# A memory-value chain moved ahead of value loads, weights taken one pair earlier, a comparison moved to GpSimd

## The chip, the cores and the metric

The kernel runs on one core of a Trainium2 chip. Its metric is the device time of one execution, in microseconds (us). Three runs of the kernel before took 1214.63, 1216.63 and 1217.8 us; the median is 1216.63. The profile is of one execution of its own.

## The reference

Two independent layers share the input length of 2048 positions; their outputs are put side by side.

Layer A is a state-space scan: `h = Lam_bar * h + x @ B_bar` over the positions, and `y = 2 * Re(h @ C) + x * D`.

Layer B is attention in 64 segments of 32 positions, with 32 heads of 128 elements and 8 memory rows:

```python
for s in range(n_seg):
    h = concatenate([mem, xs], axis=1)            # 8 memory rows, 32 positions
    q, k, v = h @ Wq, h @ Wk, h @ Wv
    p = softmax(where(mask, q @ k.T * scale, -1e9))
    o = (p @ v) @ Wo
    mem = o[:, :M]                                # the next segment's memory
    outs.append(o[:, M:])
```

The memory rows of a segment come from the segment before. The kernel does not run the segments one after another. It first makes a guess of every segment's memory (`guess`, kept as columns of `b_xe` behind the inputs, called memT), computes all segments with it, and in the end holds statistics gathered on the way (`b_cert`, `b_nrm`, `b_accE`, `b_rall`) against limits; if they do not hold, a general loop is run instead. "Guess comparison" means the part of these statistics that each block of heads adds.

## The kernel before

The work runs in this order; the times are those of the profile.

- To 346 us: values `v = x @ Wv` of all blocks of four heads (hb 0 to 7), interleaved with stage 1 of layer A. Values go to DRAM as `b_vx`.
- 346 to 464 us: stage 2 of layer A, and the guess.
- 464 to about 985 us, the stage of the change: `proj` makes queries and keys for 16 pairs of heads (hp), and `attention` works on one pair while `proj` makes the next. Each pair of heads has 18 projection steps, of eight or 32 matmuls (L578 and L589), and nine attention units, u = 0 to 8. Two projection steps go between two units, and ten go ahead of the first unit. `v_mem(hb)` computes the values of the memory rows once for each block of four heads.
- From 985 us: the output projection with Wo, which runs to the end.

`v_mem` is a generator of three pieces. The first loads the block's weights (wv), multiplies them with memT (32 matmuls, L488), copies the result to `b_vmst` on ScalarE (ACT, L492 by the helper's line 74, and L493), and stores it to DRAM as `b_vm` (L494). The second loads it back transposed as `b_vmr` (L497), squares two things on ACT into `b_wide` (L500, L501), and subtracts them into `b_ct` on VectorE (DVE, L503): this is the guess comparison. The third stores `b_vt` to DRAM (L505) and sums `b_ct` over the partitions on TensorE (`sums`: L515, read out by L516). Block 0 is taken between the first ten projection steps, after those numbered 2, 5 and 8; block hp + 1 is taken during head pair hp, at units 3, 5 and 7.

`load_v(i)` loads, for half i of the units, the values `b_v` (one transfer of 512 KB, L602) and the memory values `b_u` (four of 128 KB, L607, which read `b_vt`). An attention unit scores (L626), takes exponentials on ACT (L628), masks on GpSimd (POOL, L635), multiplies with `b_v` (L666), adds `b_u` on DVE (L668), takes reciprocals (L670), and scales on POOL (L674).

All these transfers are issued on one queue, that of SyncE (SP). Weights of every kind come into one pool of six buffers of 1 MB (`w8`): wqk of a pair (two transfers, L554), wv of a block (L383), and in the stages before those of C and Wo. All projection steps, `v_mem` and `sums` share two PSUM buffers, psP. Copies of queries and keys out of psP are done by DVE and ACT through one helper (lines 74 and 76). At the end of a pair two short steps (L589) are copied by four DVE casts (L592, L593, again line 76).

The order of the instructions on each engine is set when the program is built. A scheduler goes through the traced program and gives each engine its next instruction: the first in program order among those whose inputs and buffer are there. So a load can be issued long before its place in the text. `keep_in_program_order` (`pin` in the code) ties an instruction behind the one that was traced before it on its engine; it is only an order, not a wait.

The loop that drives the stage is this:

```python
pr, at = b.proj(), b.attention()
vm = b.v_mem(0)
for i in range(done):
    next(pr)
    if i in (2, 5, 8):
        next(vm)
```

Of the kernel before, what the change touches and what calls it, by code (L numbers as in the profile page):

```python
# [12 lines left out]
ALU = mybir.AluOpType  # L13
# [13 lines left out]
HB = 8; HP = 16  # L27
# [265 lines left out]
class PartB:  # L293
# [186 lines left out]
    def v_mem(self, hb):  # L480

        k = self.k
        pin = k.tc.keep_in_program_order
        w = self.load_wv(hb)
        p = k.ps("P")
        for h in range(4):
            for c in range(KC):
                k.PE.matmul(p[:, h * NM:(h + 1) * NM], w[:, c, h * 128:(h + 1) * 128], self.memT[:, c, :],  # L488
                            start=(c == 0), stop=(c == KC - 1))
        st = self.vmst[hb % 2]  # L490
        pv = p[:, 0:4 * NM].rearrange("p (h n) -> p h n", h=4)
        k.copy("s", st[:, :, 0:M], pv[:, :, 0:M])  # L492
        k.S.activation(st[:, :, M:NM], pv[:, :, M:NM], ACT.Copy, scale=float(M))  # L493
        pin(k.SP.dma_start(self.vm[hb].rearrange("(h p) n -> p h n", p=128), st[:]))  # L494
        yield
        vr = self.p3.tile([128, 512], BF16, name="b_vmr", bufs=1)
        pin(k.SP.dma_start(vr[:], self.vm[hb][:, :], transpose=True))  # L497
        n = NSEG - 2
        a, b = (self.wide[:, 4 * n * i:4 * n * i + 4 * n].rearrange("p (h n) -> p h n", h=4) for i in range(2))
        k.S.activation(a, self.ogT[:, hb * 4:(hb + 1) * 4, 1:1 + n], ACT.Square, scale=TOL)  # L500
        k.S.activation(b, st[:, :, M:M + n], ACT.Square, scale=1.0 / L)  # L501
        t = self.ct[:, hb % 2, 0:4 * n]
        k.V.tensor_tensor(t.rearrange("p (h n) -> p h n", h=4), a, b, ALU.subtract)  # L503
        yield
        pin(k.SP.dma_start(self.vt[hb][:], vr[0:NM, :]))  # L505
        self.sums(self.ct[:, hb % 2, :], 2 * hb)
        yield
# [42 lines left out]
    def load_wqk(self, hp):  # L550
        if hp < HP:
            w = self.k.w8((2 * KC, 256), "wqk")
            for i in range(2):
                self.k.SP.dma_start(w[:, i * KC:(i + 1) * KC, :], self.Wf[i][:, :, hp * 256:(hp + 1) * 256])  # L554
            self.wqk[hp] = w

    def norm(self, hp, w, i, hh):
# [7 lines left out]
    def proj(self):  # L565

        k = self.k; PE = k.PE
        NS = T + M - XMAIN
        for hp in range(HP):
            self.load_wqk(hp + 1)  # L570
            w = self.wqk.pop(hp)
            for q in range(4):
                for i in range(2):
                    t = self.qk[hp % 2][i]
                    for hh in range(2):
                        p = k.ps("P")
                        for c in range(KC):
                            PE.matmul(p[:, 0:480], w[:, i * KC + c, hh * 128:(hh + 1) * 128], self.xe[:, c, 480 * q:480 * q + 480],  # L578
                                      start=(c == 0), stop=(c == KC - 1))
                        k.copy("s" if i else "v", t[:, hh, M + 480 * q:M + 480 * q + 480], p[:, 0:480])  # L580
                        if q == 1:
                            self.norm(hp, w, i, hh)
                        yield
            for i in range(2):
                t = self.qk[hp % 2][i]
                p = k.ps("P")
                for hh in range(2):
                    for c in range(KC):
                        PE.matmul(p[:, hh * NS:(hh + 1) * NS], w[:, i * KC + c, hh * 128:(hh + 1) * 128], self.xe[:, c, XMAIN:XMAIN + NS],  # L589
                                  start=(c == 0), stop=(c == KC - 1))  # L590
                pv = p[:, 0:2 * NS].rearrange("p (h n) -> p h n", h=2)
                k.copy("v", t[:, :, M + XMAIN:QW], pv[:, :, 0:128])  # L592
                k.copy("v", t[:, :, 0:M], pv[:, :, 128:NS])  # L593
                yield


    def load_v(self, i):
        if i < 2 * HP:
            k = self.k
            hp, half = divmod(i, 2)  # L600
            hb, cs = hp // 2, slice((hp % 2) * 256, (hp % 2) * 256 + 256)
            k.SP.dma_start(self.vb[i % 3][:, :, 1:257], self.vx[hb][1024 * half:1024 * half + 1024, :].rearrange("(g p) n -> p g n", p=128)[:, :, cs])  # L602
            v = self.vt[hb][:, :]
            for j in range(4):
                r = M - 1 + 32 * half + j
                src = bass.AP(v.tensor, v.offset + r * 512 + (hp % 2) * 256, [[0, 32], [4 * 512, NU], [1, 256]])
                k.SP.dma_start(self.ub[i % 3][32 * j:32 * j + 32, :, 1:257], src)  # L607

    def load_vs(self, hb):
        k = self.k  # L610
# [72 lines left out]

    def attention(self):
        units = [(hp, u) for hp in range(HP) for u in range(UPH)]
        self.load_v(0)
        self.load_v(1)
        pend = []
        for n, (hp, u) in enumerate(units):
            if u == 1:  # L690
                self.load_v(2 * hp + 2)
            if u == 3 and hp % 2 == 0:
                self.load_vs(hp // 2)
            if u == 6:
                self.load_v(2 * hp + 3)
            pend.append((hp, u, self.att_front(hp, u)))
            if len(pend) > 2:
                self.att_back(*pend.pop(0))
            yield hp, u
        for p in pend:  # L700
            self.att_back(*p)
            yield HP, 0
# [202 lines left out]
def kernel_main(tc, A_x, A_Lre, A_Lim, A_Bre, A_Bim, A_Cre, A_Cim, A_logdt, A_Dskip, B_x, B_mem0, B_Wq, B_Wk, B_Wv, B_Wo, out,  # L905
                force=False, dbg=None):
    with ExitStack() as ctx:
        k = K(tc, ctx)
# [3 lines left out]
        a = PartA(k, A_x, A_Lre, A_Lim, A_Bre, A_Bim, A_Cre, A_Cim, A_logdt, A_Dskip, out)  # L912
        b = PartB(k, B_x, B_mem0, B_Wq, B_Wk, B_Wv, B_Wo, out)

        def pool(name, side, bufs=2):
            return tc.tile_pool(name=name, bufs=bufs, side=side, reuse_waits="tile")
# [7 lines left out]
        with pool("p1", "right") as p1:  # L924
# [26 lines left out]
            def values():  # L951
                yield from b.v_first(wvs[0], xr, k.SP)
                for hb, q in [(1, 0), (1, 1)] + [(hb, q) for q in range(2, 8) for hb in range(2)]:
                    yield from b.v_pair(hb, q, wvs[hb], k.SP)
                for hb in range(2, HB):
                    for q in range(8):
                        if q == 1 and hb + 1 < HB and hb + 1 not in wvs:
                            wvs[hb + 1] = b.load_wv(hb + 1)
                        yield from b.v_pair(hb, q, wvs[hb], k.SP)
            v = values()  # L960
# [17 lines left out]
            for n in range(PC * NB):  # L978
# [8 lines left out]
                half = done + 2  # L987
# [32 lines left out]
        with pool("p2", "right") as p2:  # L1020
            g = b.guess()
# [17 lines left out]
        with pool("p3", "right") as p3:  # L1039
            b.p3 = p3  # L1040
            b.qk_init(p3)
            pr, at = b.proj(), b.attention()
            vm = b.v_mem(0)
            done = 10
            for i in range(done):
                next(pr)
                if i in (2, 5, 8):
                    next(vm)
            b.wo0, b.acc = [], {}
            early = b.op_some([(0, 0), (1, 0)], range(3), "P", 2)  # L1050
            for n, (hp, u) in enumerate(at):
                if u == 3 and hp < 7:
                    vm = b.v_mem(hp + 1)
                if u in (3, 5, 7) and hp < 7:
                    next(vm)
                if u == 4 and 8 <= hp < 12:
                    w = k.w8((8, 512), "wo0")
                    k.SP.dma_start(w, b.Wo[:, 8 * (hp - 8):8 * (hp - 7), 0:512])
                    b.wo0.append(w)
                if u == 6 and hp in (4, 8, 12):  # L1060
                    b.load_o(0, hp // 4 - 1)
                want = min(18 * HP, 10 + 2 * (n + 1))
                if done == want:
                    for _ in range(2):
                        next(early, None)
                while done < want:
                    next(pr)
                    done += 1
                    if done == 18 * HP:
                        w1 = xep.tile([128, KC, XP], BF16, name="b_xe")  # L1070
                        b.wo1 = w1[:].rearrange("p c n -> p (c n)")[:, 0:H * 512].rearrange("p (h n) -> p h n", h=H)
                        k.SP.dma_start(b.wo1, b.Wo[:, :, 512:D])
            for _ in early:
                pass
# [101 lines left out]
```

## Time and profile before

| | |
|---|---|
| median of three runs | 1216.63 us (1214.63 to 1217.8) |
| the profiled execution | 1214.49 us |
| its span, first to last instruction | 1212.8 us |
| granted TensorE clock, mean | 0.999 |
| TensorE (PE) busy | 1202.6 us |
| VectorE (DVE) busy | 591.1 us |
| ScalarE (ACT) busy | 392.9 us |
| GpSimd (POOL) busy | 323.0 us |
| share of the 16 DMA engines, 464 to 500 us | 0.85 |

How to read the lines shown from here on: in a timeline, a line has its start and its duration in us, the engine, the line of the kernel, the operation, what it writes and reads with shapes, and how many instructions were merged into it; in square brackets stands how long the engine had been idle before it and what ended that. A line of SPq is a transfer's issue on the SP queue, not the transfer. In the waits, a line has the engine and what waited, for what, the us in total, how many times, and the longest.

### The profile page before, as it was taken

How to read it: one execution, taken by the hardware profiler on the slowest of the kernel's cores; microseconds unless marked ns; L12 is line 12 of the kernel's file. 1: busy time of each engine (PE TensorE's matmuls, PEld its weight loads, DVE VectorE, ACT ScalarE, POOL GpSimd, SP SyncE). 2: the span in 40 equal slices, each digit the busy share in tenths (PEclk: the TensorE clock that was granted, in tenths of full speed). 3: DMA queues.
4: the chain of work that ended last, by engine and by line, in shares of the span. 5: the costliest groups of instructions: out<-in, count | busy, mean ns of one | idle time of the engine just before them, and what ended most of it. 6: DMA issues, size and time to landing. Idle time of an engine off the chain costs nothing.

```text
span 1212.8 us, 18965 instructions
## 1 busy us (share of the span) xinstructions
PE 1202.6 (99%) x7592; PEld 621.5 (51%) x7592; DVE 591.1 (49%) x1012; ACT 392.9 (32%) x841; POOL 323.0 (27%) x345
## 2 busy tenths in 40 slices
PE   9999999999999999999999999999999999999998
PEld 4444444444445544555555555555555554444444
DVE  5889999999973333343444344444444440100000
ACT  3444344443320003444444444444444420000000
POOL 1000000000023232455555555555555560000000
PEclk9999999999999999999999999999999999999999
DMA  9932232432666646987678775755575559507000
GB/s 233 280 113 61 96 96 61 104 96 57 145 184 206 210 140 182 152 218 173 164 148 192 164 183 135 170 133 131 131 162 137 107 192 214 147 18 156 18 26 19
DMA packets 334004, 168.42 MB, mean 139 GB/s; under 512 B 144712, under 2 KB 327744, under 8 KB 333896
## 3 DMA queue, kind: packets, MB, share of 16 engines
q1 hardware_dynamic: 331832, 165.33, 55.0%
q10 hardware_dynamic: 2080, 1.84, 0.5%
q8 instruction: 61, 1.00, 0.4%
q14 instruction: 31, 0.25, 0.1%
HBM read 89.74 MB, written 43.70 MB: 110 GB/s over the span
## 4 chain that ended last, share of the span: by engine, by line
PE 96%; DMA 2%; DVE 1%; ACT 0%; issue 0%; SPq 0%; DVEq 0%
PE psP L578 33%; PE psS L722 10%; PE psP L391 9%; PE psS L391 9%; PE psO L232 9%; PE psP L722 5%; PE psP L286 5%; PE psS L286 5%; PE psO L666 2%; PE psO L722 2%; PE psS L626 2%; PE psP L589 1%; PE psS L755 1%; DVE b_ct L503 1%; DMA b_vt<-b_vmr 1%; PE psO L470 1%
## 5 line engine op out<-in xcount | busy, mean ns | idle before, releaser
L578 PE MATMUL psP<-b_xe,w 128*128 128x480 bf16 x2048 | 433.6, 366 | 4.3 <-DVE b_q L76 4.3
L578 PEld LDWEIGHTS <-w 128*128 128x128 bf16 x2048 | 195.6, 98 | 196.3 <-issue 3.1
L635 POOL TENSOR_TENSOR b_m<-b_e,maskX 128x512 bf16<-128x512 bf16 x128 | 147.8, 1155 | 228.8 <-ACT b_e L628 217.8
L391 PEld LDWEIGHTS <-b_xe 128*128 128x128 bf16 x1024 | 99.7, 98 | 119.1 <-DVE b_xe L76 0.3
L76 DVE CAST b_q<-psP 128x480 bf16<-128x480 f32 (+2 forms) x160 | 92.2, 584 | 140.5 <-PE psP L578 136.5
L74 ACT ACTIVATE b_k<-psP 128x480 bf16<-128x480 f32 x128 | 73.1, 571 | 242.5 <-PE psP L578 242.3
L722 PEld LDWEIGHTS <-b_ol 128*128 128x128 bf16 x960 | 93.5, 98 | 111.3
L668 DVE TENSOR_TENSOR b_s<-psO,b_u 128x516 f32<-128x516 f32 x128 | 88.2, 689 | 115.5 <-PE psO L666 101.0
L674 POOL TENSOR_TENSOR b_ot<-b_s,b_rall 128x512 bf16<-128x512 f32 x128 | 133.0, 1041 | 21.3 <-DVE b_rall L670 21.3
L628 ACT ACTIVATE b_e<-psS 128x512 bf16<-128x512 f32 x144 | 79.7, 554 | 158.4 <-PE psS L626 153.2
L232 PE MATMUL psO<-w,a_bt 128*128 128x512 bf16 x512 | 115.7, 379 | 0.0
L332 POOL MEMSET b_z<- 8x128 bf16 x1 | 0.2, 195 | 346.3 <-DVE a_hs L268 346.3
L722 PE MATMUL psS<-w,b_ol 128*128 128x512 bf16 x416 | 92.3, 379 | 0.0
L391 PE MATMUL psS<-w,b_xe 128*128 128x512 bf16 x384 | 90.7, 379 | 0.0
L391 PE MATMUL psP<-w,b_xe 128*128 128x512 bf16 x384 | 90.7, 379 | 0.0
L232 PEld LDWEIGHTS <-a_bt 128*128 128x128 bf16 x512 | 49.7, 98 | 59.0
L286 PEld LDWEIGHTS <-a_hs 128*128 128x128 bf16 x512 | 49.5, 98 | 58.3
L76 DVE CAST b_ost<-psS 128x512 bf16<-128x512 f32 x13 | 9.0, 692 | 138.6 <-PE psS L722 138.6
L562 ACT ACTIVATE b_wide<-w 128x1024 bf16<-128x1024 bf16 x64 | 67.3, 1052 | 0.5
L74 ACT ACTIVATE b_vst<-psS 128x512 bf16<-128x512 f32 x56 | 33.4, 597 | 96.1 <-PE psS L391 80.2
L74 ACT ACTIVATE b_vst<-psP 128x512 bf16<-128x512 f32 x56 | 33.4, 597 | 83.8 <-PE psP L391 77.6
L286 PE MATMUL psS<-w,a_hs 128*128 128x512 bf16 x256 | 57.9, 379 | 0.0
(197 smaller groups left out, 1214.3 us busy)
## 6 DMA issues: line engine op xcount, KB each, us to landing
b_v<-b_vx SPq DMA_DIRECT2D x32, 512.0 KB
b_u<-b_vt SPq DMA_DIRECT2D x128, 128.0 KB
b_vx<-b_vst SPq DMA_DIRECT2D x56, 256.0 KB
w<-in_B_Wv_dram SPq DMA_DIRECT2D x14, 1024.0 KB
w<-in_B_Wo_dram SPq DMA_DIRECT2D x12, 1024.0 KB
w<-in_B_Wq_dram SPq DMA_DIRECT2D x16, 512.0 KB
w<-in_B_Wk_dram SPq DMA_DIRECT2D x16, 512.0 KB
b_os<-b_ot SPq DMA_DIRECT2D x16, 512.0 KB
```

The costliest lines, as they stand in the source:

```text
L74: self.S.activation(out, in_, ACT.Copy)
L76: self.V.tensor_copy(out, in_)
L232: m = PE.matmul(u[:, i, :], self.bt[:, i, c, :], self.xT[tb][:, c, :], start=(c == 0), stop=(c == KC - 1))
L286: PE.matmul(py[:], self.hs[tb][:, pc, i, tt * 128:(tt + 1) * 128], self.ct[half, i][:, pc, :], start=(pc == 0 and i == 0), stop=(pc == PC ...
L391: m = self.k.PE.matmul(p[:], self.xe[:, c, t * 128:(t + 1) * 128], w[:, c, :], start=(c == 0), stop=(c == KC - 1))
L562: k.tc.keep_in_program_order(k.S.activation(wide, w[:, i * KC:(i + 1) * KC, hh * 128:(hh + 1) * 128], ACT.Square, accum_out=self.nrm[:, n: ...
L578: PE.matmul(p[:, 0:480], w[:, i * KC + c, hh * 128:(hh + 1) * 128], self.xe[:, c, 480 * q:480 * q + 480], start=(c == 0), stop=(c == KC - 1))
L628: k.S.activation(e[:, 0:nj * n], s[:, 0:nj * n], ACT.Exp, scale=float(E) ** -0.5, accum_out=self.accE[:, i:i + 1])
L635: k.G.tensor_tensor(m[:], ev, k.maskX[:].unsqueeze(1).to_broadcast([128, nj, n]), ALU.mult)
L668: V.tensor_tensor(s[:], o[:, :, 0:VW], ut[:, 2 * v:2 * v + 2, :], ALU.add)
L674: k.G.tensor_tensor(ot[:, 2 * v:2 * v + 2, :].rearrange("p g (h e) -> p g h e", h=2), s[:, :, 1:257].rearrange("p g (h e) -> p g h e", h=2 ...
L722: k.PE.matmul(self.acc[t, half], ol[:, h8, tt * 128:(tt + 1) * 128], self.wo_half(half, h), start=(h == 0), stop=(h == H - 1))
```

## The change

Five things are changed.

- The matmuls of `v_mem(0)` are taken before the first projection step; its second and third pieces come after steps 0 and 2. `load_v` is split into `load_v` (values) and `load_u` (memory values). For the first halves they are called from the driving loop: b_v(0) behind the store of b_vm, b_u(0) and b_v(1) behind the store of b_vt, b_u(1) after step 5.
- The transfers of b_v and b_u for halves 0, 1 and 2, and those of the weights of head pair 1, are pinned in program order.
- The weights of the next pair are loaded at that pair's fifth projection step (q == 1) and no longer ahead of its first.
- `v_mem` gives way once behind its weight load. The weights of blocks 0 and 1 are asked for ahead of everything, those of block hp + 2 at unit 4 of pair hp.
- The subtraction that makes `b_ct` runs on GpSimd and no longer on VectorE.

```diff
@@ v_mem
         w = self.load_wv(hb)
+        yield
         p = k.ps("P")
...
-        k.V.tensor_tensor(t.rearrange("p (h n) -> p h n", h=4), a, b, ALU.subtract)
+        k.G.tensor_tensor(t.rearrange("p (h n) -> p h n", h=4), a, b, ALU.subtract)
@@ load_wqk
-                self.k.SP.dma_start(w[:, i * KC:(i + 1) * KC, :], self.Wf[i][:, :, hp * 256:(hp + 1) * 256])
+                d = self.k.SP.dma_start(w[:, i * KC:(i + 1) * KC, :], self.Wf[i][:, :, hp * 256:(hp + 1) * 256])
+                if hp == 1:
+                    self.k.tc.keep_in_program_order(d)
@@ proj
-            self.load_wqk(hp + 1)
             w = self.wqk.pop(hp)
             for q in range(4):
+                if q == 1:
+                    self.load_wqk(hp + 1)
@@ load_v
-            k.SP.dma_start(self.vb[i % 3][:, :, 1:257], self.vx[hb][1024 * half:1024 * half + 1024, :].rearrange("(g p) n -> p g n", p=128)[:, :, cs])
-            v = self.vt[hb][:, :]
+            d = k.SP.dma_start(self.vb[i % 3][:, :, 1:257],
+                               self.vx[hb][1024 * half:1024 * half + 1024, :].rearrange("(g p) n -> p g n", p=128)[:, :, cs])
+            if i < 3:
+                k.tc.keep_in_program_order(d)
+
+    def load_u(self, i):
+        if i < 2 * HP:
+            k = self.k
+            hp, half = divmod(i, 2)
+            v = self.vt[hp // 2][:, :]
             for j in range(4):
                 r = M - 1 + 32 * half + j
                 src = bass.AP(v.tensor, v.offset + r * 512 + (hp % 2) * 256, [[0, 32], [4 * 512, NU], [1, 256]])
-                k.SP.dma_start(self.ub[i % 3][32 * j:32 * j + 32, :, 1:257], src)
+                d = k.SP.dma_start(self.ub[i % 3][32 * j:32 * j + 32, :, 1:257], src)
+                if i < 3:
+                    k.tc.keep_in_program_order(d)
@@ attention
-        self.load_v(0)
-        self.load_v(1)
...
             if u == 1:
                 self.load_v(2 * hp + 2)
+                self.load_u(2 * hp + 2)
...
             if u == 6:
                 self.load_v(2 * hp + 3)
+                self.load_u(2 * hp + 3)
@@ kernel_main
-            vm = b.v_mem(0)
+            vms = [b.v_mem(hb) for hb in range(HB)]
+            for hb in range(2):
+                next(vms[hb])
+            vm = vms[0]
             done = 10
+            next(vm)
+            b.load_v(0)
             for i in range(done):
                 next(pr)
-                if i in (2, 5, 8):
+                if i in (0, 2):
                     next(vm)
+                if i == 2:
+                    b.load_u(0)
+                    b.load_v(1)
+                if i == 5:
+                    b.load_u(1)
...
-                if u == 3 and hp < 7:
-                    vm = b.v_mem(hp + 1)
                 if u in (3, 5, 7) and hp < 7:
-                    next(vm)
+                    next(vms[hp + 1])
+                if u == 4 and hp < 6:
+                    next(vms[hp + 2])
```

## The prediction

> **What bounds the kernel now.** I read the page's first part, then the waits of TensorE, then the timeline of the places where TensorE stood still, then the timeline of the SP queue there.
>
> ```profile
> span 1212.8 us, 18965 instructions
> PE 1202.6 (99%) x7592; PEld 621.5 (51%) x7592; DVE 591.1 (49%) x1012; ACT 392.9 (32%) x841; POOL 323.0 (27%) x345
> ```
>
> TensorE is busy for 1202.6 of 1212.8 us. The change removes no matmul and adds none, so all it can move is the rest, 10.2 us. By windows, 0.85 us of that lies in the first 40 us and 5.05 us after 1100 (5.05 = 113.00 - 107.95), both untouched. Between 464 and 985 us, the attention stage, 4.6 us are left (2.23 + 2.32 in two windows, none after 700). The waits of TensorE name whom it waited for:
>
> ```profile
> PE psP L578 <- DVE b_q L76: 4.3, 8, 1.7
> PE psO L666 <- DVE b_s L668: 0.3, 1, 0.3
> ```
>
> So the ceiling of this change is 4.6 us, 0.38% of the time. The eight waits fall into three kinds. First, the edge between head pairs 0 and 1:
>
> ```profile
> 495.91 0.69 DVE L668 TENSOR_TENSOR b_s<-psO,b_u 128x516 f32<-128x516 f32 x1 [6.13 <-DMA b_u<-b_vt]
> 496.66 0.39 PE L666 MATMUL psO<-b_v,b_m 128*128 128x129 bf16 x4 [0.26 <-DVE b_s L668]
> 497.53 0.68 DVE L503 TENSOR_TENSOR b_ct<-b_wide 128x248 bf16<-128x248 f32 x1
> 498.13 0.49 DVE L76 CAST b_q<-psP 128x256 bf16<-128x256 f32 x2
> 498.77 3.40 PE L578 MATMUL psP<-b_xe,w 128*128 128x480 bf16 x16 [1.72 <-DVE b_q L76]
> ```
>
> DVE stood 6.13 us at the first L668, whose memory values b_u had not landed; its casts of b_q stood behind that, and TensorE behind the casts: 0.26 + 1.72 = 1.98 us. Second, six later edges (pairs 1 to 6), 2.3 us together, of this form:
>
> ```profile
> 530.30 1.04 POOL L674 TENSOR_TENSOR b_ot<-b_s,b_rall 128x512 bf16<-128x512 f32 x1
> 530.41 1.21 DVE L503 TENSOR_TENSOR b_ct<-b_wide 128x248 bf16<-128x248 f32 x1 [0.65 <-ACT b_wide L501]
> 531.54 0.49 DVE L76 CAST b_q<-psP 128x256 bf16<-128x256 f32 x2
> 532.09 3.41 PE L578 MATMUL psP<-b_xe,w 128*128 128x480 bf16 x16 [0.31 <-DVE b_q L76]
> ```
>
> There the comparison L503 holds up the casts. Third, 0.25 us at 480.83, where the column sums (L515) had taken one of the two psP buffers and the next step had to wait for a cast. Why b_u was late stands on the SP queue:
>
> ```profile
> 466.19 0.85 SPq L383 DMA_DIRECT2D w<-in_B_Wv_dram  x1
> 467.13 4.27 SPq L602 DMA_DIRECT2D b_v<-b_vx  x2
> 471.51 2.78 SPq L494 DMA_DIRECT2D b_vm<-b_vmst  x1
> 478.83 1.20 SPq L497 DMA_TRANSPOSE b_vmr<-b_vm  x1
> 481.49 0.27 SPq L505 DMA_DIRECT2D b_vt<-b_vmr  x1
> 489.02 7.08 SPq L607 DMA_DIRECT2D b_u<-b_vt  x12
> ```
>
> By the chain that ended last: b_vm took 7.3 us to land, the transpose 2.6, b_vt 7.5, and b_u landed at 495.8. b_vm had two value loads (1 MB) and two weight loads (2 MB) ahead of it.
>
> **The change part by part.**
>
> *Chain ahead of the values.* The matmuls of v_mem(0) move from behind the third projection step to before the first. Weights and memT are there (the load was issued at 422). They end at 464.46 + 1.05 = 465.5 instead of 470.4, their copies on ACT (some 0.5 us) at 466.0. SP is at its weight loads until 467.0, and the two value loads no longer come between: b_vm goes out at about 467.0, 4.5 us earlier. At unchanged prices for the three transfers b_u(0) lands at 495.8 - 4.5 = 491.3; with 1 MB less ahead (the records show 311 to 356 GB/s there, so 3 us) at about 488. What is needed? Without its stalls TensorE would start pair 1 at 498.77 - 1.98 = 496.8. From landing DVE needs L668, L670, L668, L670 and the casts of b_q, by the chain 0.71 + 0.18 + 0.59 + 0.18 + 0.43, about 2.2 us with gaps. So b_u has to be there by 494.6. Both ends, 488 and 491.3, are. **1.98 us go.** b_v(0) now follows b_vm: issued near 467.5, read first by L666 at 489.15, so 20 us cover it; without them each us of delay would be one of TensorE.
>
> *SP now waits in order* at L497, L505 and L607 for the transfer before, and b_v(1), pair 1's weights, b_u(1), b_v(2) and b_u(2) are pinned behind them. b_v(1) and b_u(1) are read half a pair later, after 502. Pair 1's weights are the ones at risk: before, they were issued at 410 and 411, 85 us early. In the new order they follow b_u(0), so they go out at 486 to 488. Their price is that of the pair issued at 480.12: its first half's packets were through 3.4 us after issue, all 5.2 us after. With b_u(0) and b_v(1) ahead, 4 us more: 491 to 495, needed at 497.1 (496.8, and 0.35 for the sums' move below). In time, with little to spare, if a buffer is free. The six w8 buffers are handed out as they come free: before, wqk(2) and wv(2) were issued at 464.27 and 466.19, as stage 2 gave back its last two. The loads that are not pinned (wv(2), wqk(2), wv(3)) may take those that wqk(1) would have had; then it waits for wv(1)'s, given back by v_mem(1) at 494.5, lands half at 494.5 + 3.4 = 497.9, and costs 497.9 - 497.1 = 0.8 us. So 0 to 0.8. I take 0: TensorE has other work (memory-value matmuls of 1.05 us, scores at 0.22) which can be ordered into such a hole, as eight L626 were at 479.97.
>
> *Sums of block 0* move from behind the ninth step to behind the third. There is no attention work yet to lie beside them. Behind step 9, TensorE ran 0.6 us of L626 and then idled 0.25. Now the old 0.25 goes, and the step after the sums waits until ACT has cleared the third step (0.57 us and two gaps, less the sums' own time): 0.6 us. Bounds: 0 if other work is put in, 0.85 from the sum of the row of before. **Cost 0.6, gain 0.25.**
>
> *Comparison on GpSimd.* The row of before: 1.21 us in six of eight, 0.41 at 475.83 where POOL was idle. At 530.41 DVE started while L674 ran (530.30 to 531.34), and finished 0.3 us after it. The Trainium skill speaks against the move: "GPSIMD Engine Reference", section 4.1, calls two-input elementwise work about twice as slow there as on VectorE. By that it would be 0.8 us. By rows: L635 takes 1155 ns for 512 elements, the 80-element L632 337 ns, so 1.9 ns per element and 0.65 us for 248. And "SBUF — State Buffer", Who interferes with whom, says that a DVE instruction with two SBUF inputs and a GpSimd one that reads SBUF exclude each other for a whole instruction. The collision row agrees (0.41 alone, 1.21 beside L674): what counts is not 0.41 against 0.65, but that DVE loses 1.2 us just ahead of the casts. On POOL it runs behind L674, in the 1.06 us that POOL idles before the next L635 (531.34 to 532.40): 0.65 or 0.8, both fit. Were that cover gone, L635 would be up to 0.8 us later, and its reader is two units (7 us) behind. L515 reads b_ct 12 us later; L562, which rewrites b_wide, comes 8 us later. Next late after the casts: L589's second half (1.03) and L626, L666 (0.46) lie between the first half and L578, 1.5 us for casts of 0.4 us, even behind one L668 and L670 (0.9). **2.3 us go.** No edge after 700, where there is no L503, has a wait: this is the direct evidence.
>
> *Weights one pair ahead.* wv was already loaded far ahead (issued at 466.19, read at 528): 0 either way, but for the buffers above.
>
> **Sum.** 1.98 + 2.3 + 0.25 - 0.6 = 3.9 us. The profiled execution took 1214.49 us, its span 1212.8 and 1.7 around it; it would become 1210.6. The median of the three runs is 2.1 us above it: 1216.63 - 3.9 = **1212.7 us** (0.32%). A measurement can tell about 0.3%, 3.65 us, so this sits at the edge.
>
> **The rivals.**
>
> *Pair 1's weights wait for a buffer (0.26).* For it: loads were handed out as soon as buffers came free, and now one load is held back. Against: work to fill the hole. -3.9 + 0.8 = -3.1: 1213.5.
>
> *The chain is still late (0.15).* If further weight loads of 1 MB each (3 us apiece) get ahead of b_vm and b_vt, b_u lands after 494.6 and up to 1.98 us stay: 1214.6.
>
> *Slower (0.09).* One mechanism: pair 1's weights get no buffer until pair 0's is given back (L589's end, 496.5) and another pair's 1 MB lies ahead: 496.5 + 5.2 + 3.4 = 505.1, 8.0 us of bare wait at 497.1, 1216.63 - 3.9 + 8.0 = 1220.7. It decides from 3.9 us on: the first half landing after 501.0, so issued alone after 497.6.
>
> *As forecast (0.50).* So faster by over 0.3%: 0.50; within: 0.26 + 0.15 = 0.41; slower: 0.09. The range goes from all 4.5 us gained with 1.3 us of scatter, 1210.8, to the late chain with 1 us of scatter, 1215.6 (the runs of before spread over 3.2 us).
>
> **What would show it.** In the new profile: no TensorE wait at the edges of pairs 1 to 6 and L503 on POOL at 0.5 to 0.8 us; b_vm issued near 467 and the first b_u landed before 494.6, DVE's wait at L668 under 3 us; a new wait of about 0.6 us near 470; TensorE idle between 464 and 985 down to 0.6. Wrong if LDWEIGHTS of L578 waits for a weight DMA near 497, or if the busy time of TensorE itself changes.

## The result and the profile after

The kernel after took 1209.38 us (median of four runs, 1209.24 to 1209.67), the kernel before beside it 1215.63 us (four runs, 1213.85 to 1217.8). The ratio is 0.9948, with a 95% interval of 0.9930 to 0.9966: 0.5% less, and below the predicted range of 1210.8 to 1215.6. The profiled execution took 1209.38 us, where that of before took 1214.49.

The page's first part and the waits of TensorE, of the kernel after (its line numbers are a few higher: the projection is L582 and L593, the memory values L489, the sums L516 with their copy L517, the comparison L504, the addition of b_u L682):

```profile
span 1207.7 us, 18958 instructions
PE 1201.4 (99%) x7592; PEld 621.7 (51%) x7592; DVE 584.7 (48%) x1004; ACT 393.0 (33%) x841; POOL 327.9 (27%) x353
```

```profile
PE psS L419 <- PEq L1181: 0.8, 1, 0.8
PE psP L582 <- DVE b_cert L517: 0.3, 1, 0.3
```

The first wait is at the start of the program, outside the change. In the attention stage one wait of 0.27 us is left of nine. But the busy time fell too, by 1.2 us, with the same 7592 matmuls. The prediction had named that as a sign against it; the experiments below take it up.

The SP queue of after:

```profile
466.24 0.39 SPq L495 DMA_DIRECT2D b_vm<-b_vmst  x1
466.74 1.66 SPq L606 DMA_DIRECT2D b_v<-b_vx  x1
...
473.35 0.26 SPq L506 DMA_DIRECT2D b_vt<-b_vmr  x1
478.08 1.82 SPq L619 DMA_DIRECT2D b_u<-b_vt  x4
...
480.44 0.58 SPq L555 DMA_DIRECT2D w<-in_B_Wq_dram  x1
481.06 3.21 SPq L555 DMA_DIRECT2D w<-in_B_Wk_dram  x1
```

b_vm goes out at 466.24 (predicted: near 467), b_u at 478.08 instead of 489.02. Between 464 and 480 no weight load stands in this queue; before, wqk(2) and wv(2) were issued at 464.27 and 466.19. So not 1 MB but 3 MB are gone from ahead of b_vm, and pair 1's weights are issued at 480.4, not at 486 to 488. The timeline of DVE at the first edge, and of TensorE at the sums and at the edge:

```profile
489.90 0.69 DVE L682 TENSOR_TENSOR b_s<-psO,b_u 128x516 f32<-128x516 f32 x1
...
495.47 0.51 DVE L76 CAST b_q<-psP 128x256 bf16<-128x256 f32 x2 [1.08 <-PE psP L593]
```

```profile
470.40 0.19 PE L516 MATMUL psP<-const-bfloat16-1.0,b_ct 128*128 128x1 bf16 x2
470.86 11.50 PE L582 MATMUL psP<-b_xe,w 128*128 128x480 bf16 x56 [0.27 <-DVE b_cert L517]
...
496.67 3.40 PE L582 MATMUL psP<-b_xe,w 128*128 128x480 bf16 x16
```

L682 no longer waits for a transfer: before, it stood 6.13 us. DVE's casts of b_q stand 2.7 us earlier, and TensorE goes into pair 1 without a gap. At a later edge (end of pair 1), the timeline of GpSimd:

```profile
528.20 1.04 POOL L688 TENSOR_TENSOR b_ot<-b_s,b_rall 128x512 bf16<-128x512 f32 x1
529.20 0.71 POOL L504 TENSOR_TENSOR b_ct<-b_wide 128x248 bf16<-128x248 f32 x1
530.31 1.15 POOL L649 TENSOR_TENSOR b_m<-b_e,maskX 128x512 bf16<-128x512 bf16 x1 [0.40 <-ACT b_e L642]
```

The comparison takes 0.71 us there, lies behind L688 in what was idle time, and 0.40 us of that is left ahead of the mask (L649).

### The profile page after: what moved, and what is told of

It reads as the page before. It is cut to its first block, busy times and chain, and to the rows that moved or that the text cites. A ratio compares the mean times of both kernels' runs of the same rounds, so it can differ in the third digit from the quotient of the medians.

```text
span 1207.7 us, 18958 instructions
## 1 busy us (share of the span) xinstructions
PE 1201.4 (99%) x7592; PEld 621.7 (51%) x7592; DVE 584.7 (48%) x1004; ACT 393.0 (33%) x841; POOL 327.9 (27%) x353
## 4 chain that ended last, share of the span: by engine, by line
PE 99%; DVE 0%; issue 0%
PE psP L582 34%; PE psS L736 10%; PE psS L391 9%; PE psP L391 9%; PE psO L232 9%; PE psP L736 5%; PE psP L286 5%; PE psS L286 5%; PE psP L593 3%; PE psO L680 2%; PE psS L640 2%; PE psO L736 2%; PE psS L769 1%; PE psP L489 1%; PE psO L470 1%; PE psP L456 0%
## 5 line engine op out<-in xcount | busy, mean ns | idle before, releaser
L582 PE MATMUL psP<-b_xe,w 128*128 128x480 bf16 x2048 | 433.8, 366 | 0.3 <-DVE b_cert L517 0.3
L582 PEld LDWEIGHTS <-w 128*128 128x128 bf16 x2048 | 195.7, 98 | 190.7 <-issue 0.3
L649 POOL TENSOR_TENSOR b_m<-b_e,maskX 128x512 bf16<-128x512 bf16 x128 | 147.5, 1152 | 223.3 <-ACT b_e L642 211.1
L682 DVE TENSOR_TENSOR b_s<-psO,b_u 128x516 f32<-128x516 f32 x128 | 88.3, 690 | 112.0 <-PE psO L680 103.4
L688 POOL TENSOR_TENSOR b_ot<-b_s,b_rall 128x512 bf16<-128x512 f32 x128 | 132.8, 1040 | 15.7 <-DVE b_rall L684 15.6
```

The source lines that it names most:

```text
L649: k.G.tensor_tensor(m[:], ev, k.maskX[:].unsqueeze(1).to_broadcast([128, nj, n]), ALU.mult)
L682: V.tensor_tensor(s[:], o[:, :, 0:VW], ut[:, 2 * v:2 * v + 2, :], ALU.add)
L688: k.G.tensor_tensor(ot[:, 2 * v:2 * v + 2, :].rearrange("p g (h e) -> p g h e", h=2), s[:, :, 1:257].rearrange("p g (h e) -> p g h e", h=2 ...
```

## The experiments

**The question.** By its own sum the change had 4.6 us to win in the stage, and won more. The stage is taken here from the end of the last matmul of stage 2 of layer A to the end of the last matmul of attention (464.46 to 996.62 us in before, so with the last attention units, which lie beside the first steps of the output projection). "Idle" are the gaps in TensorE's record above 0.06 us, n their number; all are worked out from the trace. The page's busy time can't serve for this: in several runs, e1 and e2 among them, 68 matmul records of the earlier and later parts are missing. What follows the stage took 211.33 us up to the last matmul in every kernel.

| kernel | stage, us | n | idle, us | stage less idle |
|---|---|---|---|---|
| before | 532.16 | 9 | 4.55 | 527.62 |
| after | 526.56 | 1 | 0.27 | 526.30 |
| e1: comparison on GpSimd alone | 529.24 | 3 | 2.60 | 526.64 |
| e2: order of loads alone | 530.48 | 8 | 3.06 | 527.42 |
| e3: pair 1's weights not pinned | 526.56 | 1 | 0.26 | 526.30 |
| e4: values ahead of the chain | 526.57 | 1 | 0.26 | 526.30 |
| e5: comparison three times | 530.49 | 8 | 3.07 | 527.42 |
| e6: one psP buffer for four pairs | 575.68 | 67 | 38.17 | 537.52 |
| e7: sums later | 526.23 | 0 | 0.00 | 526.23 |
| e8: weights at their use | 539.65 | 8 | 9.12 | 530.54 |
| e9: e3 and e4 together | 527.45 | 2 | 0.97 | 526.47 |
| e10: long comparison on DVE | 532.54 | 15 | 3.98 | 528.56 |

**The theories.** R: each wait of TensorE costs its idle time and 0.165 us more, which the profile counts as busy, because behind a wait the first matmul shows its whole length instead of its spacing. The 0.165 is the difference of before and after, 1.32 us, over eight waits. P: the hidden part goes with the idle time, 0.31 us for each us (1.32 for 4.28). C: the busy time doesn't hang on the waits at all. R can be read off the chain of before, at the edge of pair 1 and one step later:

```profile
532.09 3.41 PE psP L578 x16
...
535.96 3.24 PE psP L578 x16
```

Sixteen matmuls of the same form take 3.24 us behind other work and 3.41 behind the wait. In the chain of after, the group behind that edge is of the first kind:

```profile
529.68 3.24 PE psP L582 x16
```

One spacing is 3.24 / 16 = 0.2025 us, and the mean length of one such matmul in the groups of both kernels is 0.366: 0.164 more. The Trainium skill has a formula for each ("TensorE: Matmul & The Clock Gate", Single matmul latency and Back-to-back issue gap). As estimates for 480 columns they give 366 and 202.5 ns, and the trace agrees with both. The page calls the second that of an isolated gap, which is too long for wide matmuls in a stream with weight loads; in this stream, with a weight load for each matmul, it holds.

One caution: the ends of matmuls in these profiles are modelled, and nearly all matmuls of this form are drawn with the same 0.366 us. So how a wait is shared out between idle and busy is the profile's doing. What the runs measure is the length of the stage, and R is tested on that.

### One part alone: e1 and e2

e1 is the kernel before with this line alone:

```diff
-        k.V.tensor_tensor(t.rearrange("p (h n) -> p h n", h=4), a, b, ALU.subtract)
+        k.G.tensor_tensor(t.rearrange("p (h n) -> p h n", h=4), a, b, ALU.subtract)
```

> The kernel before, with the subtraction that makes b_ct on GpSimd and nothing else. Theory R (a wait of TensorE costs its idle time and, hidden in its busy time, 0.16 us more, because the first matmul behind the wait shows its whole length again): the six edges of pairs 1 to 6 go, 2.3 us of idle and 6 x 0.16 = 1.0 us of busy, so TensorE busy 1201.5 to 1201.7, the span 3.2 to 3.9 us below 1212.8 (some of the first edge's 1.72 us may go as well). Rival C (the 1.1 us by which the busy time fell has nothing to do with waits): busy stays 1202.5 or falls by another amount, span 2.3 us lower. Theory S (the scatter of the kernel before, 1213.9 to 1217.8, is that of the late b_u): this kernel keeps the late b_u and scatters by over 2 us.

It took 1213.03 us (eight runs, 1210.74 to 1214.95); the kernel before, beside it, 1217.04 (14 runs, 1214.72 to 1219.36): ratio 0.9968 (0.9955 to 0.9982). The waits of TensorE in the stage (the shorter of the two for b_q is that of the sums, 0.25 us in before), and DVE at the first edge:

```profile
PE psP L578 <- DVE b_q L76: 1.4, 2, 1.1
PE psO L666 <- DVE b_s L668: 1.2, 1, 1.2
```

```profile
497.18 0.70 DVE L668 TENSOR_TENSOR b_s<-psO,b_u 128x516 f32<-128x516 f32 x1 [7.12 <-DMA b_u<-b_vt]
```

The six later edges are gone; the first one is still there, with b_u even later than in the profile of before (as in b2 below, of the kernel before itself). So the span is 2.7 us below that of before and not 3.2 to 3.9. Six waits fewer took 0.98 us of the stage without its idle time (R: 6 x 0.165 = 0.99). The runs spread over 4.2 us, as theory S had it.

e2 is the kernel after with the comparison back on DVE, so the order of the loads alone:

```diff
-        k.G.tensor_tensor(t.rearrange("p (h n) -> p h n", h=4), a, b, ALU.subtract)
+        k.V.tensor_tensor(t.rearrange("p (h n) -> p h n", h=4), a, b, ALU.subtract)
```

> The changed kernel with the subtraction back on VectorE. Theory R: the first edge (1.98) and most of the 0.25 go, the six edges come back: idle in the attention stage 2.3 + 0.3 (up to 0.4 more if pair 0's edge now waits for the subtraction as well), TensorE busy 1201.4 + 6 or 7 x 0.16 = 1202.4 to 1202.6, span 3.3 to 3.9 us above the changed kernel's 1207.7. Rival C: busy stays 1201.4, span 2.3 to 2.7 above. Theory S: the late b_u is gone, so the runs lie within 1 us of each other.

1213.24 us (six runs, 1212.59 to 1213.57), ratio 0.9967 (0.9955 to 0.9979). Its waits in the stage, and DVE at the end of pair 0:

```profile
PE psP L582 <- DVE b_q L76: 2.8, 7, 0.4
...
PE psP L582 <- DVE b_cert L517: 0.3, 1, 0.3
```

```profile
495.52 1.20 DVE L504 TENSOR_TENSOR b_ct<-b_wide 128x248 bf16<-128x248 f32 x1 [1.08 <-ACT b_wide L502]
496.65 0.49 DVE L76 CAST b_q<-psP 128x256 bf16<-128x256 f32 x2
```

Seven edges and not six: with b_u in time, the comparison at the end of pair 0 collides like the others, where before the late b_u had covered it. So each part uncovers or covers a little of the other's. In the stage the two gain 2.9 (e1) and 1.7 us (e2), and both together 5.6 (after): of the 1.0 us between, 0.56 are the seventh edge with its hidden part, and 0.37 the longer first edge of e1. In time the two gains, 4.0 and 3.8 us, add up to 7.8, where e3 and e4, which have both parts, lie 8.1 and 8.0 us below the same runs of before; there the long runs of before come in, as shown further down.

### Which order matters: e3, e4 and e9

e3 takes the pin from pair 1's weights, e4 puts both value loads ahead of the chain again, e9 does both.

```diff
@@ e3, e9
                 d = self.k.SP.dma_start(w[:, i * KC:(i + 1) * KC, :], self.Wf[i][:, :, hp * 256:(hp + 1) * 256])
-                if hp == 1:
-                    self.k.tc.keep_in_program_order(d)
@@ e4, e9
-            next(vm)
             b.load_v(0)
+            b.load_v(1)
+            next(vm)
...
                     b.load_u(0)
-                    b.load_v(1)
```

> The changed kernel without the pin on the weights of pair 1. In the order of this kernel those weights go out in stage 2 again, and wv(2) and wqk(2), 2 MB, go out just ahead of b_vm. Theory by the record's sum (the chain may land up to 494.6): b_u lands near 488 to 491, no wait of TensorE, the time within 0.3 us of the changed kernel's. Rival (the pin is what does it): b_u lands after 494.6, DVE waits over 5 us at L682 and TensorE up to 2 us; time up to 2.5 us longer and scattered again.

1208.97 us (five runs, 1208.71 to 1209.12), ratio 0.9931 (0.9917 to 0.9945): the time of after. But its SP queue is another one:

```profile
466.06 0.39 SPq L555 DMA_DIRECT2D w<-in_B_Wq_dram  x1
...
468.18 3.15 SPq L495 DMA_DIRECT2D b_vm<-b_vmst  x1
...
484.53 1.80 SPq L617 DMA_DIRECT2D b_u<-b_vt  x4
```

```profile
491.25 0.69 DVE L680 TENSOR_TENSOR b_s<-psO,b_u 128x516 f32<-128x516 f32 x1 [1.13 <-DMA b_u<-b_vt]
```

Without the pin the weight loads go out at 464.6 to 468 as before, 2 MB ahead of b_vm, and b_u lands at 491.2. The prediction had worked out 491.3 at unchanged prices; that this agrees to 0.1 us is luck, since b_vm goes out 1.2 us later than it had it, and the transfers behind it take 1.2 us less. So it is the pin on pair 1's weights that held back the loads behind it, which aren't pinned. The reason, which fits e8 below as well, is that the buffers of the weight pool go out in the order of the program, so that a load whose predecessor waits has none. That b_u is issued 6.4 us later than in after costs nothing, since it still lands ahead of 494.6.

> The changed kernel with both value loads of pair 0 (1 MB) ahead of b_vm on the queue, weights still held back. Theory by the record's sum: b_vm lands 3 us later than in the changed kernel, b_u by some 3 to 5 us, still before 490; no wait, the time within 0.3 us of the changed kernel's. Rival (the order against the values is what does it): a DVE wait at L682 of several us and a TensorE wait near 496, 0.5 to 2 us longer.

1209.06 us (five runs, 1208.57 to 1209.19), ratio 0.9932 (0.9918 to 0.9945). b_vm goes out at 468.21, b_u at 480.85, and nothing waits.

> The changed kernel with both value loads of pair 0 ahead of b_vm and without the pin on pair 1's weights, so that 3 MB lie ahead of it as before; what stays of the chain's part of the change is that v_mem(0) is computed before the projection. Of the two single returns, one had b_u at 491.2 and the other well before 490, with no wait of TensorE. Theory L (TensorE waits from the moment b_u lands after 494.6): b_vm goes out near 471, b_u lands between 493 and 496, so a wait of 0 to 1.5 us in the profile, and run times that scatter by 1 to 3 us again. Rival (the order on the queue is of no matter, only the early computation): as the changed kernel, within 0.3 us and within 0.5 us of each other.

1209.47 us (six runs, 1208.80 to 1209.93), ratio 0.9939 (0.9924 to 0.9954). With 3 MB ahead of it b_vm goes out at 472.65, and DVE and TensorE at the first edge are:

```profile
495.36 0.70 DVE L680 TENSOR_TENSOR b_s<-psO,b_u 128x516 f32<-128x516 f32 x1 [5.41 <-DMA b_u<-b_vt]
```

```profile
497.51 1.79 PE L580 MATMUL psP<-b_xe,w 128*128 128x480 bf16 x8 [0.71 <-DVE b_q L76]
```

Here b_u comes 0.76 us after 494.6, and TensorE waits 0.71 us: the threshold of the prediction holds to 0.05 us. So the early computation of the memory values does most of it: with the old order on the queue it takes the stage from 529.24 (e1) to 527.45 us. Of the two other parts, the pin on pair 1's weights and the place of the value loads, one is enough for the 0.9 us that are left; either may go at no cost. In the time of the whole kernel these 0.9 us can't be told. No run leaves out the early computation alone.

### The comparison made longer: e5 and e10

e5 repeats the subtraction on DVE (the repeats write the same values); e10 puts a long reduction, whose result is not used, ahead of it on DVE.

```diff
@@ e5
-        k.G.tensor_tensor(t.rearrange("p (h n) -> p h n", h=4), a, b, ALU.subtract)
+        for _ in range(3):
+            k.V.tensor_tensor(t.rearrange("p (h n) -> p h n", h=4), a, b, ALU.subtract)
@@ e10
...
+        wb = self.wide[:, 0:8 * n].unsqueeze(1).to_broadcast([128, 4, 8 * n])
+        k.V.tensor_reduce(self.big1[:, hb:hb + 1], wb, AX.XY, ALU.max)
-        k.G.tensor_tensor(t.rearrange("p (h n) -> p h n", h=4), a, b, ALU.subtract)
+        k.V.tensor_tensor(t.rearrange("p (h n) -> p h n", h=4), a, b, ALU.subtract)
```

> The changed kernel with the subtraction on VectorE and done three times over, so that each edge's wait is longer, but the number of waits stays at about 8. Measured from the last stage-2 matmul to the last matmul of attention, without TensorE's idle time, the runs so far give 526.30 us with 1 wait, 526.64 with 3, 527.42 with 8, 527.62 with 9. Theory R (0.16 us a wait, whatever its length): 527.4 to 527.6 with 8 or 9 waits, while the idle time grows from 3.1 to 9 us or more. Rival P (a hidden share that grows with the idle time, 0.29 us for each us): 528.7 or more.

One run, 1213.19 us, and the stage of e2 to 0.01 us. It tells nothing: only the first subtraction stands ahead of the casts, the scheduler put the other two behind them (by the timeline, casts of b_q at 530.01, the two at 530.43). The waits didn't lengthen.

> The changed kernel with the subtraction on VectorE and a long reduction of b_wide ahead of it (one input from the state buffer, some 2.1 us, its result is not used), which stands ahead of the casts of b_q at seven edges. The waits get longer by 0.9 us or so, their number stays 8. Theory R (0.165 us a wait, whatever its length): the stage without its idle time 527.4 to 527.6, while the idle time grows to 8 us or more. Rival P (0.29 us for each us of idle): 528.5 or more.

One run, 1214.71 us. DVE at the edge of pair 1:

```profile
528.96 2.22 DVE L506 TENSOR_REDUCE b_big<-b_wide 128x1 f32<-128x1984 f32 x1 [1.00 <-ACT b_wide L503]
531.10 0.50 DVE L76 CAST b_q<-psP 128x256 bf16<-128x256 f32 x2
```

The 2.2 us are there, ahead of the casts, but not the eight long waits that were expected: the order of TensorE's work changed with them, and 15 short ones came, 3.98 us in all. Seven of these are of 0.14 us, each ahead of a score. By that it tells R from P better than planned. With 526.13 for a stage without a wait (526.30 of after, less 0.165), R gives 526.13 + 15 x 0.165 = 528.6 for the stage less its idle time. P has 526.22 without a wait (526.30 less 0.31 x 0.27), and gives 526.22 + 0.31 x 3.98 = 527.5. Measured: 528.56.

### Many waits: e6

In pairs 8 to 11 one psP buffer is held by a matmul that is not used, so that all projections share the other.

```diff
             w = self.wqk.pop(hp)
+            if hp == 8:
+                hold = k.ps("P")
+                k.tc.keep_in_program_order(PE.matmul(hold[:, 0:1], k.ident[:], k.ident[:, 0:1], start=True, stop=True))
+            if hp == 12:
+                held = k.cst.tile([128, 1], FP32, name="held")
+                k.tc.keep_in_program_order(k.V.tensor_copy(held[:], hold[:, 0:1]))
```

> The changed kernel with one of the two psP buffers held back during head pairs 8 to 11, so that nearly each of their 72 steps has to wait for the copy of the one before (one tiny matmul and one tiny copy are added). Theory R: as many waits as the profile counts, n, and the stage without idle time at 526.13 + 0.165 n us, so 537 to 539 for n from 65 to 75, give or take 0.3. Rival C (the hidden part has to do with these few edges only): about 526.3 to 527.

One run, 1258.76 us; 67 waits, 38.17 us idle, and 537.52 us without it. R gives 526.13 + 67 x 0.165 = 537.2. P happens to give much the same here (526.22 + 0.31 x 38.17 = 538.1), so e6 excludes only C; e10 excludes P, and so do e1 (P 527.0, R 526.63, measured 526.64) and e2 (P 527.2, R 527.45, measured 527.42).

### The sums later: e7

The sums of a block become a piece of their own; for block 0 it is taken in the attention of pair 0, where other matmuls lie beside it, and for the other blocks where it was.

```diff
         pin(k.SP.dma_start(self.vt[hb][:], vr[0:NM, :]))
+        yield
         self.sums(self.ct[:, hb % 2, :], 2 * hb)
@@ kernel_main
+                if u == 7 and hp < 7:
+                    next(vms[hp + 1])
+                if u == 1 and hp == 0:
+                    next(vms[0])
```

> The changed kernel with the sums taken off the third piece: those of block 0 go from behind the third projection step to unit 1 of pair 0, where attention matmuls lie beside them; the store of b_vt stays where it is. Theory R: the last wait of the stage, 0.27 us of idle, goes with its 0.16, so the stage takes 526.13 us, 0.43 less, and no wait is left; time 0.3 to 0.5 us below the changed kernel's, which is hardly more than the scatter. Rival (the sums wait wherever they stand): stage 526.5.

1208.97 us (six runs, 1208.70 to 1209.76), ratio 0.9937 (0.9922 to 0.9952). No wait is left in the stage, which is 0.33 us shorter than in after (R: 0.27 + 0.165 = 0.43; so a stage without a wait is 526.23 here, 0.1 above R's 526.13). In the time of the whole kernel that can't be told from after; in the stage this version has no wait left to win.

### Weights at their use: e8

The change loads the weights of the next block a pair ahead; e8 keeps all else and asks for them at their use.

```diff
-        w = self.load_wv(hb)
         yield
+        w = self.load_wv(hb)
         p = k.ps("P")
```

> The changed kernel with the value weights asked for at their use again, all pins kept. The record's sum says 0 for this part. But buffers of the weight pool go out in program order, and pair 1's weights are pinned behind b_u(0): so wv(1), now asked for after them, goes out behind vs(0), near 495, and is needed at 493.4. Theory: the weights land near 500, TensorE waits 5 to 7 us once near 493 to 497, and the time is 4 to 7 us above the changed kernel's 1209.4. By the record (0): within 0.3 us of it.

1221.35 us (four runs, 1218.62 to 1221.76), ratio 1.0047 (1.0030 to 1.0063) to the kernel before beside it (1214.89, seven runs), and 12 us above after: more than the 4 to 7 us expected. The SP queue, TensorE, and one of its waits:

```profile
494.75 0.57 SPq L383 DMA_DIRECT2D w<-in_B_Wv_dram  x1
```

```profile
504.55 2.10 PE L489 MATMUL psP<-b_xe,w 128*128 128x71 bf16 x32 [3.58 <-DMA w<-in_B_Wv_dram]
```

```profile
PE psO L680 <- POOL b_m L649: 4.4, 4, 2.6
```

The weights of block 1, behind the pinned loads, go out at 494.75 (in after at 422.45) and hold up TensorE. The wait for the weights is there, if later and shorter than expected. But four more waits, 4.4 us together, are for GpSimd's masks: with no projections between them the attention units bunch, and GpSimd has no break. With that comes a second loss. In the windows at this place the columns are the stretch, its length, the busy time of PE, PEld, DVE, ACT and POOL (with counts), the granted clock, the DMA share and GB/s:

```profile
492.00:496.00 4.00, 2.50 (x31) 1.82 (x29) 1.96 (x5) 2.60 (x8) 2.21 (x3) 1.00 1.28 175
496.00:500.00 4.00, 1.13 (x10) 0.70 (x10) 1.19 (x5) 0.45 (x2) 4.00 (x5) 0.60 1.27 132
500.00:504.00 4.00, 0.61 (x4) 0.35 (x4) 1.57 (x4) 0.00 (x0) 4.00 (x5) 0.50 1.09 313
504.00:508.00 4.00, 3.45 (x46) 3.45 (x47) 0.00 (x0) 0.88 (x3) 0.61 (x2) 0.50 0.86 208
508.00:512.00 4.00, 4.00 (x30) 3.01 (x28) 1.01 (x4) 2.30 (x4) 0.39 (x1) 0.70 1.36 132
```

TensorE has 1.1 and 0.6 us of work in 4 where GpSimd has 4.0; the granted clock is 0.5 from 496.8 to 510.4, and the 32 matmuls of L489 take 2.10 us instead of the 1.20 of after. Of the stage's 13.1 us above after, 8.85 are idle time and 1.15 are seven waits by R. The remaining 3.1 us are put down to the low clock; they were not measured apart.

### The kernel before again: b1 and b2

Two more single runs of the unchanged kernel before, each with a profile, to see what its scatter is.

> The kernel before, unchanged, for another profile of it. Theory S (its runs differ by when b_u lands): the device time of this execution less the 1214.49 of the first profile is the start of the first L668 behind its wait less the 495.91 of the first profile, within 0.5 us, and TensorE's idle time near 496 grows or shrinks with it. Rival (the scatter has another source): the two differ by more than 1 us.

> The kernel before once more, the same expectation as for the other repetition.

b1 took 1214.65 us, with the stage of the first profile to 0.02 us. b2 took 1215.83; DVE at the first edge, and the window there (columns as in e8):

```profile
497.35 0.70 DVE L668 TENSOR_TENSOR b_s<-psO,b_u 128x516 f32<-128x516 f32 x1 [6.77 <-DMA b_u<-b_vt]
```

```profile
496.00:500.00 4.00, 1.59 (x25) 1.28 (x22) 2.58 (x8) 0.71 (x3) 1.67 (x2) 1.00 1.31 130
```

Of its 1.34 us above the first profile, 0.64 are a longer stage (b_u later), and 0.79 an earlier part that ended later (less 0.1 at the end). The expectation's sum comes out (1.34 against 497.35 - 495.91 = 1.44), but the greater part of it has nothing to do with b_u, so this is weak evidence for S. For R it is a clean test: the same nine waits with 0.63 us more of idle time leave the same 527.62 us without it, where P would have 0.2 more.

Neither run is one of the long ones, up to 1219.66, so their profile is missing. What every run has is its mean granted clock, to 0.001. Of the 32 runs of before that stand beside the experiments, all 19 from 1215.85 us up show 0.998 or 0.997, and all 13 up to 1215.34 show 0.999 or 1.000. e1, the other kernel with the late b_u, has the same split (five runs from 1212.86 up, three up to 1211.81). The 32 runs of after, e2, e3, e4, e7 and e9 all show 0.999 or 1.000, and each of these kernels scatters by 0.4 to 1.1 us. That holds for e9 too, whose b_u is late again (495.36), but costs TensorE only 0.71 us.

## Why the prediction was wrong

Two terms of the prediction's sum failed: the offset of 2.1 us, which was carried over and went, and the busy time, which was taken as fixed and fell by 0.165 us with each wait. A third, the cost of the sums, was too high by 0.33 us. The paragraphs below take them in the order of the argument.

**The three sources of gain were right.** The first edge: b_u lands ahead of 494.6, DVE doesn't wait, 1.98 us go. Of these 0.40 went only because the comparison left DVE as well (the seventh edge of e2), which the prediction had not seen. The later edges: the comparison takes 0.71 us on GpSimd, against 0.65 by rows and 0.8 by the Trainium skill's "GPSIMD Engine Reference", section 4.1; it lies inside idle time, and all six waits are gone; e1 shows them apart. The sums: the old 0.25 goes.

**"TensorE is busy for 1202.6 of 1212.8 us … all it can move is the rest."** This step failed. A part of the busy time belongs to the waits: 0.165 us each, as e1, e2, e10 and b2 show. The ceiling was 4.55 + 9 x 0.165 = 6.0 us, not 4.6; with eight waits fewer, 1.32 us were left out of the sum. The sign was on the page: 3.41 against 3.24 us for like groups of the chain.

**"The step after the sums waits until ACT has cleared the third step … 0.6 us."** It waited 0.27. The next step took the buffer of the sums themselves, which DVE frees with a small copy (L517); the third step's buffer, which ACT clears, was for the step after.

**"The median of the three runs is 2.1 us above it: 1216.63 - 3.9 …"** This is the largest part of the miss. I took the 2.1 us for something that stays, and gave no reason. It was no accident of three runs (the median of the 32 runs of before is 1216.3), but it went: profile to profile the gain is 1214.49 - 1209.38 = 5.1 us, from the median it is 7.25. The offset is made by the long runs of before. They end with the new order of loads (e2: spread of 1.0 us) and stay without it (e1: 4.2 us), and their clock is lower; that much is shown. Why the old order has them stays open. The likely reading is that in such a run b_u is later still, the first edge costs more than the profile of a short run shows, and the clock falls in the longer gap as in e8; in b2 TensorE had only 1.59 us of work in 4 there, at full clock still. No profile of a long run shows it.

The sum of the miss, 1212.7 - 1209.4 = 3.3 us: 2.1 for the offset, 1.3 for the hidden part of eight waits, 0.35 for the sums and rounding, less 0.5, since in the profiles of after the stage began 0.2 us later and the program ended 0.3 us later behind its last matmul. The range failed by the same two steps: its low end was "all 4.5 us gained with 1.3 us of scatter", 1.4 us above what was measured. The offset alone is more than that, the hidden part alone a little less.

**"The loads that are not pinned … may take those that wqk(1) would have had."** The contrary holds: the pin kept them back as well (after against e3). So the rival of pair 1's weights waiting, and the slower one built on it, had no ground in this change, and "1 MB less ahead" was 3 MB. None of this moved the time, as the spare was there either way.

**"Weights one pair ahead … 0 either way, but for the buffers above."** In the kernel before that may be so. Beside the pins it is not: e8 shows 12 us. A slower case did exist, but in a change that left this part out.

## What to carry over

Count the waits of the bounding engine as well as their length: a matmul behind a wait shows its whole length, and the difference to its spacing (0.164 us here) stands in the profile as busy time. If a kernel's runs scatter and the profile was taken in a short one, find what scatters before you subtract from the median. If the change removes it, the change is worth more than the profile says. When one load is tied to its place, look at what waits behind it for the same pool, and ask for those earlier.

## What the hardware showed besides

- The granted clock fell to 0.5 in e8 at 496.8, where TensorE had been working in short bursts with gaps of 0.3 to 0.9 us (2.50 us of work in the 4 us to 496). It stayed there through gaps of 2.6 and 3.6 us, and came back at 510.4, some 6 us after dense work had resumed (504.55). In e6, with 67 gaps of at most 1.4 us, it stayed at 1.0 all through the four pairs, where TensorE was busy for over half of any 4 us. So it was a sparse stretch and not the sum of idle time (38 us in e6, 9 in e8). How sparse and for how long isn't shown: in b2 the clock held through 4 us with 1.59 us of work.
- A comparison of 248 elements per partition took 0.71 us on GpSimd, in eight of eight. On VectorE it took 0.41 us alone, and 1.2 us in the six of eight where it started while a GpSimd scaling of 512 elements (L674) was running; it ended 0.3 us behind that.
